# Lead of an attention and two-MLP kernel: copies spread over three engines, first products in halves

## The chip, the cores and the metric

One core of one Trainium2 chip. The metric is the device time of one execution in microseconds. The median of three runs of the kernel before is 594.18 us (593.97 to 595.03).

## The reference

For 2 batches, 8 heads, 768 positions and 64 dimensions a head, each query attends to the keys within 15 positions and to 24 block summaries (the maximum of each 32 keys; the mean of their 32 values). The result, 1536 tokens of 512, goes through two MLPs.

```python
scores_l_m = np.where(mask_l, scale * q @ k.T, -1e9)          # |i - j| < 16
scores_s = scale * q @ k_sum.T + np.log(block)
a = softmax(concat[scores_l_m, scores_s])
x = a @ concat[v, v_sum]                                       # (1536, 512)
h = np.maximum(x @ w_in, 0.0);  x = h * h @ w_out              # 512 -> 2048 -> 512
h = x @ w_in2;  return (h * sigmoid(h)) @ w_out2
```

The weights arrive as 8-byte numbers and are turned into 4-byte ones in the kernel.

## The kernel before, in words

Attention works in 24 tiles of 64 queries; a tile's scores are 4 head pairs of 128 partitions x 120 columns (96 keys of the window and 24 summaries). Every product of the MLPs is made of three passes over high and low halves of the operands (`split`). The first MLP runs over three blocks of 512 tokens, and each block over 16 chunks `s` of 128 hidden columns: `gemm1` (12 matmuls of 512 columns), relu and square on ScalarE, a split, `gemm2` (12 more). The second MLP follows.

The subject is the **lead**: the first 8 tiles (`NLEAD`), in two groups of 4 (`NGRP`). They give the 512 tokens of block 0, and before they are done no MLP product can start. Block 0's chunks are interleaved with tiles 8 to 15. A lead tile's steps, by the names in `first_order`:

- `kt`: one head pair's transposed keys from DRAM; `ksum` (L620, VectorE): their block maxima.
- `kwl` (L627, ScalarE): copies the 4 windows of a group, 128 x 384, out of `kt` into the score tile `kws`. Eight of them, (head pair, group).
- `ksl` (L632, VectorE): copies the summaries behind the windows, 128 x 96. Eight.
- `psl` (L641, PE) scores of one tile and head pair; `ttl` (L400, VectorE) adds the mask and takes the minimum; `exl` (L405, ScalarE) the exponential. 32 of each.
- `ze`, `rc`, `nt` (L425, L428, L436, VectorE): the sum's inverse and the product with it; `psa` (L442, PE) transposes; `a` (L449, ScalarE) copies out of PSUM.
- `vs` (L647, PE): value summaries of batch 0 into the PSUM tile `psv`; `vmean` (L651, ScalarE): copies them into `vlead` behind the values, 24 partitions x 2048, once for each group. `vfm` (L655, ScalarE): from there to two buffers of later tiles.
- `av` (L457, PE): attention times values; `xh` (L465, ScalarE) and `xl` (L468, VectorE): high and low part of the tokens, in `xt`.

A weight chunk's steps: `raw` (DMA, 512 KB), `sc` (L285, ScalarE), `sh` (L290, VectorE), `st2` (L293, VectorE), `hi` (L703, ScalarE), `lo` (L706, VectorE); `scr` stores the joined `wo` chunk. There are 5 buffers for raw chunks (`NRAW`), and a load waits for the `st2` five chunks earlier.

Every engine runs its instructions in program order, and so does SP, which issues the loads and stores. The program order of block 0 is made by `first_order` (L63): a list scheduler. Each step has an engine, a cost, a due time and what it depends on. It takes the engine step that can start earliest, and of the steps of that engine which can start by then the one with the earliest due time. It doesn't look ahead: a step that is ready goes before one that is more urgent and ready a moment later. The plan's times only make the order; on the chip the waits decide. GpSimd has no step in it before.

`FILL` (L47) puts 6 and 4 idle matmuls behind two of the early scores, and `WARM` 10 at the start.

Of the kernel before, what the change touches and what calls it, by code (L numbers as in the profile page):

```python
# [10 lines left out]
F32 = mybir.dt.float32  # L11
# [11 lines left out]
P = 128  # L23
# [3 lines left out]
QT = 64  # L27
NWIN = QT + 2 * WIN
NK = NWIN + NSUM
TPB = S // QT  # L30
NG = B * TPB
NHP = H // 2
NF = DFF // P
# [10 lines left out]
NVF = 2  # L44
NLEAD = 8
NGRP = 4
# [6 lines left out]
NRING = 8  # L53
FIRST2 = 1
DEC1 = 14
GROUPS = [[(0, 0, 256, 256, 0), (1, 256 * 0, 128, 128, 256)], [(1, 256, 384, 128, 0), (2, 0, 256, 256, 128)]]
STARTS = [[0, 128, 512, 256, 384, 640], [768, 1024, 1152, 896, 1280, 1408]]
CHAIN = ["11", "s1", "s2", "s4", "s3", "12", "22"]
# [4 lines left out]
def first_order():  # L63
# [6 lines left out]
    def op(eng, name, arg, dur, due, deps=(), bank=None, kb=0):  # L70
        o = index[name, arg] = dict(eng=eng, name=name, arg=arg, dur=dur, due=due + shift.get(name, 0), deps=list(deps), bank=bank, kb=kb,
                                    n=len(ops))
        ops.append(o)
# [4 lines left out]
    def tile_due(g):  # L78
        return 0.25 * g if g < NLEAD else 46 + 11 * (g - NLEAD)
# [9 lines left out]
    for hp in range(NHP):  # L89
        op("vec", "ksum", hp, 1.0, -50 + hp, [("kt", hp, 0)])  # L90
        for i in range(NLEAD // NGRP):
            op("act", "kwl", (hp, i), .5, -50 + hp + 51 * i, [("kt", hp, 0)])
            op("vec", "ksl", (hp, i), .13, -50 + hp + 48 * i, [("ksum", hp, 0)])
    for c in range(6):
        op("pe", "vs", c, .92, 2.7 + .1 * c, [("vr", c // 2, 0)])
    for i in range(NLEAD // NGRP):
        op("act", "vmean", i, 1.9, -5, [("vs", c, M) for c in range(6)] + [("vl", i, 0)] * 0)
    for i in range(NVF):
        op("act", "vfm", i, .6, tile_due(NLEAD) - 10 + i, [("vmean", 0, 0)])

    for j in range(4 * NHP):
        due = tile_due(TPB) - 20 + j
# [5 lines left out]
    for g in range(NFIRST):  # L108
        due, two = tile_due(g), g - 2 >= NLEAD
        if g < NLEAD:  # L110
            for hp in range(NHP):
                op("pe", "psl", (g, hp), .29, due, [("kwl", (hp, g // NGRP), A), ("ksl", (hp, g // NGRP), A), ("q", g // NGRP, 0)] +
                   [("psl", (g, hp - 1), 0)] * (hp > 0), bank=None if hp else ("acc", "ttl", (g, NHP - 1)))
                op("vec", "ttl", (g, hp), .21, due, [("psl", (g, hp), M), ("cst", 0, 0)])
                op("act", "exl", (g, hp), .385, due, [("ttl", (g, hp), A)])
            exp = [("exl", (g, hp), A) for hp in range(NHP)]
        else:
            load("kw", g, 246, due - 9, [("pss", g - 2, M)] * two)
            load("qr", g, 131, due - 8.9, [("pss", g - 2, M)] * two)
            load("vf", g, 196, due - 6, [("av", g - 2, M)] * two)  # L120
            op("vec", "kwc", g, .13, due - .5, [("kw", g, 0)] + [("kvr", 4 * NHP - 1, 0)] * (g >= TPB))
            if TPB <= g < TPB + NVF:
                op("vec", "vfc", g, .35, due, [("vf", g, 0), ("vendc", 0, A)])
            op("pe", "pss", g, 1.22, due, [("kwc", g, A), ("qr", g, 0)] + [("gemm1", 1, 0)] * (g == NLEAD), bank=("att", "ttr", g))
            op("vec", "ttr", g, .84, due, [("pss", g, M), ("psa", g - 2, M)])
            op("act", "exp", g, 1.54, due, [("ttr", g, -.45)])
            exp = [("exp", g, A)]
        op("vec", "ze", g, .09, due, exp)
        op("vec", "rc", g, .1, due, [("ze", g, .1)])
        op("vec", "nt", g, .78, due, [("rc", g, .1)])  # L130
        op("pe", "psa", g, .62, due - 2, [("nt", g, -.1)], bank=("att", "a", g))
        op("act", "a", g, .56, due, [("psa", g, M)] + [("av", g - 1, M)] * (g > NLEAD))
        values = [("vl", g // NGRP, 0), ("vmean", g // NGRP, A)] if g < NLEAD else [("vf", g, 0), ("vfm", g % NVF, A)]
        op("pe", "av", g, .66, due, values + [("a", g, A)] + [("vfc", g, A)] * (TPB <= g < TPB + NVF),
           bank=("acc" if g < NLEAD else "att", "xl", g))
        op("act", "xh", g, .32, due, [("av", g, M)])
        op("vec", "xl", g, .36, due, [("xh", g, A)])

    chunks = [(x, s) for s in range(NF) for x in ("wi", "wo")]
    for i, (x, s) in enumerate(chunks):  # L140
        due = chunk_due(s) - 5 + .5 * (x == "wo") - 20 * (not i)
        load("raw", (x, s), 524, chunk_due(s) - 14 + .5 * (x == "wo") - 100 * (not i),
             [("st2", chunks[i - NRAW], A)] if i >= NRAW else [])
        before = [("sc", chunks[i - 1], 0)] * (i > 0)
        if i >= NSPL:
            y = chunks[i - NSPL]
            before += [("lo", y, A)] + [("scr", y[1], 0)] * (y[0] == "wo")
        op("act", "sc", (x, s), .59, due, [("raw", (x, s), 0)] + before)
        op("vec", "sh", (x, s), .35, due, [("raw", (x, s), 0)])
        op("vec", "st2", (x, s), .61, due, [("sh", (x, s), 0), ("sc", (x, s), A)])  # L150
        if x == "wo":
            load("scr", s, 262, chunk_due(s) + 2, [("st2", (x, s), A)])
        op("act", "hi", (x, s), .57, due, [("st2", (x, s), A)] + [("gemm2", s - NWO - NXWO, M)] * (x == "wo" and s >= NWO + NXWO))
        op("vec", "lo", (x, s), .61, due, [("hi", (x, s), A)])

    for s in range(NF):
        due = chunk_due(s)
        op("pe", "gemm1", s, 2.72, due, [("xl", g, A) for g in range(NLEAD)] + [("lo", ("wi", s), A)] +
           [("relu", s - 2, A)] * (s >= 2))
        op("act", "relu", s, .57, due, [("gemm1", s, M)] + [("gl", s - 2, A)] * (s >= 2))  # L160
        op("act", "sq", s, .57, due, [("relu", s, 0)])
        op("act", "gh", s, .57, due, [("sq", s, 0)] + [("gemm2", s - 3, M)] * (s >= 3))
        op("vec", "gl", s, .61, due, [("gh", s, A)])
        op("pe", "gemm2", s, 2.72, due + 5 * LAG, [("gl", s, A), ("lo", ("wo", s), A)] + [("gemm2", s - 1, 0)] * (s > 0))

    free = dict(sp=0.0, act=0.0, vec=0.0, pe=5.6)
    end, banks, moved = {}, dict(att=[], acc=[]), 2.0
    room = dict(att=2, acc=4)

# [34 lines left out]
def kernel(  # L204
# [35 lines left out]
    def copy(eng, o, i, scale=1.0):  # L240
        if eng is act:
            return act.activation(out=o, in_=i, func=AF.Copy, scale=scale)  # L242
        return eng.tensor_copy(out=o, in_=i)  # L243
# [48 lines left out]
    def dec_join(name, c):  # L292
        vec.scalar_tensor_tensor(out=c, in0=c, scalar=3, in1=raws.pop(name)[:, :, 0],  # L293
                                 op0=ALU.logical_shift_left, op1=ALU.bitwise_or)
# [255 lines left out]
    def gemm1(w, x, c0, n, h):  # L550
        for k in range(NKC):
            ws = slice(k * P, (k + 1) * P)
            xh, xl = x[:, 0, k, c0:c0 + n], x[:, 1, k, c0:c0 + n]
            mm(h, w[:, 0, ws], xh, start=(k == 0), stop=False)
            mm(h, w[:, 0, ws], xl, start=False, stop=False)
            mm(h, w[:, 1, ws], xh, start=False, stop=(k == NKC - 1))
# [16 lines left out]
    def first_block():  # L573
# [50 lines left out]
        def kwl(hpi):  # L624
            hp, i = hpi
            w = kts[hp][:, i * NGRP * QT:i * NGRP * QT + NWIN]
            copy(act, kws[i][hp // 2][:, hp % 2, :, 0:NWIN], bass.AP(w.tensor, w.offset, [w.ap[0], [QT, NGRP], w.ap[1]]))  # L627

        def ksl(hpi):
            hp, i = hpi  # L630
            s = ksum[0][:, hp]
            copy(vec, kws[i][hp // 2][:, hp % 2, :, NWIN:NK], bass.AP(s.tensor, s.offset, [s.ap[0], [0, NGRP], s.ap[1]]))  # L632

        def psl(ghp):
            g, hp = ghp
# [12 lines left out]

        def vmean(i):
            means = psv[NWIN:NK]  # L650
            copy(act, vlead[NWIN:NK, i * NGRP:i * NGRP + NGRP].rearrange("p g h d -> p g (h d)"),  # L651
                 bass.AP(means.tensor, means.offset, [means.ap[0], [0, NGRP], means.ap[1]]))

        def vfm(i):
            copy(act, vf[i][NWIN:NK], vlead[NWIN:NK, 0])  # L655

        def kv(j):
            hp, w, i = j // 4, j // 2 % 2, j % 2
# [27 lines left out]
        def name(xs):  # L686
            return f"{xs[0]}{xs[1]}"
# [17 lines left out]
        def lo(xs):  # L705
            sub(vec, ws[xs][:, 1], cs[xs].bitcast(F32), ws[xs][:, 0].bitcast(F32))  # L706

        def gemm1_(s):
            h = hs[s] = ps_h.tile([P, 512], F32, tag="h", name=f"h0_{s}")
            gemm1(wi1[s], x, 0, 512, h)  # L710

        def relu(s):
            rs[s] = r_p.tile([P, 512], F32, tag="r", name=f"r0_{s}")
# [17 lines left out]
        def xh(g):  # L731
            if g * QT >= BLOCKS[0]:
# [6 lines left out]
                  exl=lambda a: exponential(*a), nt=lambda g: norm(g, vec),  # L739
                  psa=transposes, a=a_copy, av=products, xh=xh, xl=x_low, raw=raw, sc=sc,  # L740
                  sh=lambda xs: dec_low(name(xs)),
                  st2=lambda xs: dec_join(name(xs), cs[xs]), scr=scr_, hi=hi, lo=lo, gemm1=gemm1_, relu=relu, sq=sq, gh=gh,
                  gl=gl, gemm2=gemm2_)
        for what, arg in first_order():
            do[what](arg)
# [363 lines left out]
```

## Time and profile before

| | us |
|---|---|
| median of three runs | 594.18 |
| the profiled execution's own time | 595.07 |
| its span, first to last instruction | 593.3 |
| PE busy | 584.0 |
| VectorE busy | 388.7 |
| ScalarE busy | 367.1 |
| GpSimd busy | 88.9 |

The profiled execution is 0.89 us above the median; 1.77 us of it lie around the span. PE is TensorE's matmul row, DVE is VectorE, ACT is ScalarE, POOL is GpSimd, SP is the engine that issues DMAs. A row's "x4" counts instructions, and merged timeline rows add the lengths from the first start to the last end. On VectorE and ScalarE an instruction's recorded length runs somewhat into the next one's start, so that the spacing of starts is what one more costs.

### The profile page before, as it was taken

How to read it: one execution, taken by the hardware profiler on the slowest of the kernel's cores; microseconds unless marked ns; L12 is line 12 of the kernel's file. 1: busy time of each engine (PE TensorE's matmuls, PEld its weight loads, DVE VectorE, ACT ScalarE, POOL GpSimd, SP SyncE). 2: the span in 40 equal slices, each digit the busy share in tenths (PEclk: the TensorE clock that was granted, in tenths of full speed). 3: DMA queues.
4: the chain of work that ended last, by engine and by line, in shares of the span. 5: the costliest groups of instructions: out<-in, count | busy, mean ns of one | idle time of the engine just before them, and what ended most of it. 6: DMA issues, size and time to landing. Idle time of an engine off the chain costs nothing.

```text
span 593.3 us, 9499 instructions
## 1 busy us (share of the span) xinstructions
PE 584.0 (98%) x3300; PEld 491.9 (83%) x3300; DVE 388.7 (66%) x975; ACT 367.1 (62%) x848; POOL 88.9 (15%) x93
## 2 busy tenths in 40 slices
PE   7989999999999999999999999999999999999997
PEld 6578888887887887888888898999988998889995
DVE  5989999733756665267544676777776766666542
ACT  5999998654555655375553676566656655555532
POOL 0000000012554443156333300000000000000000
PEclk9999999999999999999999999999999999999999
DMA  8999999525598888526682112242229411111102
GB/s 308 270 290 352 345 360 339 185 83 181 189 345 303 284 269 303 211 107 206 233 274 68 36 36 89 88 144 88 84 89 378 174 39 36 31 25 35 36 19 106
DMA packets 42240, 104.42 MB, mean 176 GB/s; under 512 B 4560, under 2 KB 11856, under 8 KB 42192
## 3 DMA queue, kind: packets, MB, share of 16 engines
q1 hardware_dynamic: 42192, 103.81, 51.4%
q8 instruction: 26, 0.43, 0.3%
q14 instruction: 22, 0.18, 0.1%
HBM read 78.37 MB, written 25.43 MB: 175 GB/s over the span
## 4 chain that ended last, share of the span: by engine, by line
PE 95%; ACT 2%; DMA 1%; DVE 1%; issue 0%; SPq 0%; DVEq 0%
PE acc L238 45%; PE h L238 23%; PE hx L238 11%; PE hz L238 6%; PE pss L238 4%; PE hy L238 3%; PE psa L442 2%; PE av L238 2%; DMA t_ksum<-in_kT_dram 1%; ACT T L405 1%; PE psv L238 1%; ACT vlead L242 1%; ACT a L242 0%; ACT xt L242 0%; PE idle_out L238 0%; DVE ksum L620 0%
## 5 line engine op out<-in xcount | busy, mean ns | idle before, releaser
L238 PE MATMUL acc<-wq,g 128*128 128x512 f32 x576 | 142.4, 392 | 0.0
L238 PE MATMUL h<-xt,wi 128*128 128x512 f32 x576 | 142.2, 394 | 0.0
L238 PE MATMUL acc<-g,wo 128*128 128x512 f32 x576 | 141.1, 393 | 0.0
L238 PEld LDWEIGHTS acc<-g,wo 128*128 128x128 f32 x576 | 107.1, 188 | 23.1 <-ACT xt L242 0.2
L238 PEld LDWEIGHTS h<-xt,wi 128*128 128x128 f32 x576 | 106.3, 188 | 22.9 <-issue 0.6
L238 PEld LDWEIGHTS acc<-wq,g 128*128 128x128 f32 x576 | 107.1, 188 | 19.7 <-DVE wq L246 0.2
L246 DVE TENSOR_TENSOR g<-r,g 128x512 fp32r<-128x512 f32 x48 | 38.4, 801 | 60.5 <-ACT g L242 31.0
L246 DVE TENSOR_TENSOR r_s<-v,r_s 128x256 fp32r<-128x256 f32 x48 | 20.5, 431 | 50.2 <-ACT r_s L242 50.1
L242 ACT ACTIVATE g<-s 128x384 fp32r<-128x384 f32 x64 | 33.2, 521 | 22.0 <-DVE s L246 22.0
L246 DVE TENSOR_TENSOR g<-s,g 128x384 fp32r<-128x384 f32 x64 | 35.5, 556 | 15.1 <-ACT g L242 13.2
L405 ACT ACTIVATE T<-T,m 128x120 f32<-128x120 f32 x96 | 36.7, 384 | 11.2 <-DVE m L400 11.0
L242 ACT ACTIVATE e<-hx 128x384 f32<-128x384 f32 x32 | 15.7, 492 | 43.8 <-PE hx L238 43.8
L238 PE MATMUL hx<-x_t,r_s 128*128 128x384 f32 x192 | 38.9, 337 | 0.0
L238 PEld LDWEIGHTS hx<-x_t,r_s 128*128 128x128 f32 x192 | 34.5, 188 | 2.7
L932 ACT ACTIVATE s<-e 128x384 f32<-128x384 f32 x48 | 25.2, 525 | 15.4 <-DVE e L246 15.3
L246 DVE TENSOR_TENSOR s<-e,s 128x384 f32<-128x384 f32 x48 | 26.5, 553 | 5.2 <-ACT s L932 5.2
L526 ACT ACTIVATE r<-h 128x512 f32<-128x512 f32 x16 | 9.5, 596 | 30.9 <-PE h L238 30.9
L246 POOL TENSOR_TENSOR wo<-c_wo,wo 128x512 fp32r<-128x512 f32 x16 | 26.1, 1632 | 13.1 <-ACT wo L242 12.6
L242 ACT ACTIVATE r<-u 128x256 fp32r<-128x256 f32 x48 | 19.5, 409 | 12.7 <-PE hx L238 12.7
L243 POOL COPY qd<-qr 128x256 f32<-128x256 f32 x8 | 5.8, 719 | 133.7 <-DVE z L425 125.8
L400 DVE CUSTOM_DVE_ANT_0 T<-pss,cst_sb 128x120 f32<-128x120 f32 x96 | 21.8, 274 | 4.3 <-PE pss L238 4.0
L246 POOL TENSOR_TENSOR r<-r 128x512 f32<-128x512 f32 x16 | 17.0, 1064 | 48.6 <-ACT g L531 48.6
(112 smaller groups left out, 912.0 us busy)
## 6 DMA issues: line engine op xcount, KB each, us to landing
raw_wi<-in_w_in_dram SPq DMA_DIRECT2D x16, 512.0 KB, 5.6
raw_wo<-in_w_out_dram SPq DMA_DIRECT2D x16, 512.0 KB, 5.6
raw_wp<-in_w_out_dram SPq DMA_DIRECT2D x16, 512.0 KB, 5.4
split<-wo SPq DMA_DIRECT2D x16, 512.0 KB, 3.7
raw_wj<-in_w_in_dram SPq DMA_DIRECT2D x16, 512.0 KB, 4.6
wo<-split SPq DMA_DIRECT2D x16, 512.0 KB, 3.4
c<-scr_dram SPq DMA_DIRECT2D x32, 256.0 KB, 2.6
scr_dram<-c_wo SPq DMA_DIRECT2D x16, 256.0 KB, 4.4
```

Of the source, the lines that this page charges most:

```text
L238: pe.matmul(o, l, r, **kw)
L242: return act.activation(out=o, in_=i, func=AF.Copy, scale=scale)
L243: return eng.tensor_copy(out=o, in_=i)
L246: return eng.tensor_tensor(out=o, in0=a, in1=b, op=op)
L400: vec.tensor_tensor_reduce(out=d["T"][:, c], in0=d["ps"][:, c], in1=cst_sb[:, kind * NK:kind * NK + NK], scale=-0.125, scalar=3.0e38, op0= ...
L405: act.activation(out=d["T"][:, c], in_=d["T"][:, c], func=AF.Exp, bias=d["m"][:, c:c + 1], scale=-1.0, accum_out=d["z"][:, c:c + 1])
L442: pe.transpose(ps[0:NK, c], d["T"][:, c], id_sb)
L526: act.activation(out=r, in_=h, func=AF.Relu)
L932: act.activation(out=s, in_=src, func=AF.Sigmoid)
```

## The change

GpSimd becomes an engine of the plan. Seven of the eight `kwl` go from ScalarE to GpSimd (the first stays), all eight `ksl` from VectorE to GpSimd, both `vfm` from ScalarE to GpSimd, and the second `vmean` from ScalarE to VectorE. The first MLP product of chunks 0 and 1 is made in two halves of 256 tokens: `half1` needs only tiles 0 to 3, `gemm1` makes the rest. The chunks are ordered anew, the `wo` of a chunk 1.5 places behind its `wi` (`wi0, wi1, wo0, wi2, wo1, wi3, ...`), and the decoding of every chunk from the third on waits, in the plan, for the last lead tile's `nt`. Several of the plan's costs are changed.

```diff
+NHALF = 2
         for i in range(NLEAD // NGRP):
-            op("act", "kwl", (hp, i), .5, -50 + hp + 51 * i, [("kt", hp, 0)])
-            op("vec", "ksl", (hp, i), .13, -50 + hp + 48 * i, [("ksum", hp, 0)])
+            op("pool" if i or hp else "act", "kwl", (hp, i), .5, -50 + hp + 51 * i, [("kt", hp, 0)])
+            op("pool", "ksl", (hp, i), .25, -50 + hp + 48 * i, [("ksum", hp, A)])
     for i in range(NLEAD // NGRP):
-        op("act", "vmean", i, 1.9, -5, [("vs", c, M) for c in range(6)] + [("vl", i, 0)] * 0)
+        op("vec" if i else "act", "vmean", i, 2.2 if i else 1.85, -5, [("vs", c, M) for c in range(6)])
     for i in range(NVF):
-        op("act", "vfm", i, .6, tile_due(NLEAD) - 10 + i, [("vmean", 0, 0)])
+        op("pool", "vfm", i, .7, tile_due(NLEAD) - 10 + i, [("vmean", 0, 0)])
-                op("pe", "psl", (g, hp), .29, due, [("kwl", (hp, g // NGRP), A), ("ksl", (hp, g // NGRP), A), ("q", g // NGRP, 0)] +
+                op("pe", "psl", (g, hp), 0.2, due, [("kwl", (hp, g // NGRP), A), ("ksl", (hp, g // NGRP), A), ("q", g // NGRP, 0)] +
...
-        op("act", "a", g, .56, due, [("psa", g, M)] + [("av", g - 1, M)] * (g > NLEAD))
+        op("act", "a", g, .5, due, [("psa", g, M)] + [("av", g - 1, M)] * (g > NLEAD))
...
-        op("pe", "av", g, .66, due, values + [("a", g, A)] + [("vfc", g, A)] * (TPB <= g < TPB + NVF),
+        op("pe", "av", g, .53, due, values + [("a", g, A)] + [("vfc", g, A)] * (TPB <= g < TPB + NVF),
...
-    chunks = [(x, s) for s in range(NF) for x in ("wi", "wo")]
+    chunks = sorted(((x, s) for s in range(NF) for x in ("wi", "wo")), key=lambda c: c[1] + 1.5 * (c[0] == "wo"))
+        held = [("nt", NLEAD - 1, 0)] * (i > 1)
-        op("act", "sc", (x, s), .59, due, [("raw", (x, s), 0)] + before)
-        op("vec", "sh", (x, s), .35, due, [("raw", (x, s), 0)])
-        op("vec", "st2", (x, s), .61, due, [("sh", (x, s), 0), ("sc", (x, s), A)])
+        op("act", "sc", (x, s), .57, due, [("raw", (x, s), 0)] + before + held)
+        op("vec", "sh", (x, s), .35, due, [("raw", (x, s), 0)] + held)
+        op("vec", "st2", (x, s), .6, due, [("sh", (x, s), 0), ("sc", (x, s), A)])
-        op("pe", "gemm1", s, 2.72, due, [("xl", g, A) for g in range(NLEAD)] + [("lo", ("wi", s), A)] +
-           [("relu", s - 2, A)] * (s >= 2))
+        if s < NHALF:
+            op("pe", "half1", s, 1.45, due - 30, [("xl", g, A) for g in range(NGRP)] + [("lo", ("wi", s), A)])
+        op("pe", "gemm1", s, 1.45 if s < NHALF else 2.72, due, [("xl", g, A) for g in range(NLEAD)] + [("lo", ("wi", s), A)] +
+           [("half1", s, 0)] * (s < NHALF) + [("relu", s - 2, A)] * (s >= 2))
-    free = dict(sp=0.0, act=0.0, vec=0.0, pe=5.6)
+    free = dict(sp=0.0, act=0.0, vec=0.0, pool=2.0, pe=5.6)
...
+        def half1(s):
+            h = hs[s] = ps_h.tile([P, 512], F32, tag="h", name=f"h0_{s}")
+            gemm1(wi1[s], x, 0, 256, h[:, 0:256])
+
         def gemm1_(s):
-            h = hs[s] = ps_h.tile([P, 512], F32, tag="h", name=f"h0_{s}")
-            gemm1(wi1[s], x, 0, 512, h)
+            if s < NHALF:
+                gemm1(wi1[s], x, 256, 256, hs[s][:, 256:512])
+            else:
+                h = hs[s] = ps_h.tile([P, 512], F32, tag="h", name=f"h0_{s}")
+                gemm1(wi1[s], x, 0, 512, h)
```

In `kwl`, `ksl`, `vmean` and `vfm` only the engine of the copy changes, and `half1` joins the table of steps.

## Rows read from the trace of the kernel before

**Rows 1.** Page, parts 1 and 2: busy time by engine; the granted clock by slice.

```profile
PE 584.0 (98%) x3300; PEld 491.9 (83%) x3300; DVE 388.7 (66%) x975; ACT 367.1 (62%) x848; POOL 88.9 (15%) x93
...
PEclk9999999999999999999999999999999999999999
```

**Rows 2.** Windows: stretch, its length, each engine's busy time (instructions), clock, DMA share, GB/s.

```profile
9.12:31.06 21.94, 19.57 (x159) 12.43 (x159) 19.81 (x126) 20.51 (x79) 0.00 (x0) 1.00 1.05 304
31.06:37.44 6.38, 5.70 (x147) 5.17 (x146) 4.57 (x15) 6.32 (x14) 0.00 (x0) 1.00 0.94 260
60.00:80.00 20.00, 20.00 (x114) 16.11 (x113) 19.35 (x53) 18.12 (x40) 0.00 (x0) 1.00 0.99 350
```

**Rows 3.** Chain that ended last, in order of time: start, length, what.

```profile
28.99 3.63 ACT vlead L242 x2
36.22 1.22 PE pss L238 x16
37.44 5.67 PE h L238 x24
...
47.24 2.72 PE h L238 x12
...
333.75 1.06 PE hx L238 x6
```

**Rows 4.** ScalarE's groups from 9.7 to 29 us (columns as in the page's part 5).

```profile
L242 ACT ACTIVATE kws<-t_ksum 128x384 f32<-128x384 f32 x4 | 1.9, 510 | 0.0
```

**Rows 5.** Timeline of ScalarE: start, length, what, [idle before it <- releaser].

```profile
9.72 0.39 ACT L405 ACTIVATE T<-T,m 128x120 f32<-128x120 f32 x1 [0.55 <-DVE m L400]
...
14.80 0.38 ACT L405 ACTIVATE T<-T,m 128x120 f32<-128x120 f32 x1
...
15.18 0.38 ACT L405 ACTIVATE T<-T,m 128x120 f32<-128x120 f32 x1
...
36.01 0.64 ACT L242 ACTIVATE xt<-av 128x256 fp32r<-128x256 f32 x2
...
39.99 0.63 ACT L242 ACTIVATE vfr<-vlead 24x512 f32<-24x512 f32 x1
```

**Rows 6.** Timeline of VectorE.

```profile
8.17 0.95 DVE L620 TENSOR_REDUCE ksum<-t_ksum 128x24 f32<-128x768 f32 x1 [2.99 <-DMA t_ksum<-in_kT_dram]
...
11.76 0.33 DVE L243 COPY kws<-ksum 128x96 f32<-128x96 f32 x2
...
29.87 0.43 DVE L290 TENSOR_SCALAR raw_wi<-raw_wi 128x512 int32<-128x512 int32 x1 [0.48 <-DMA raw_wi<-in_w_in_dram]
30.21 0.85 DVE L436 TENSOR_SCALAR T<-T,r 128x120 f32<-128x120 f32 x4
...
36.75 0.75 DVE L246 TENSOR_TENSOR xt<-av,xt 128x256 fp32r<-128x256 f32 x2
...
50.22 0.68 DVE L246 TENSOR_TENSOR wi<-c_wi,wi 128x512 fp32r<-128x512 f32 x1
```

**Rows 7.** PE's waits: who waited for whom, total us, times, longest.

```profile
PE psa L442 <- DVE T L436: 1.4, 1, 1.4
```

**Rows 8.** GpSimd's groups over the whole span, shapes kept apart.

```profile
L246 POOL TENSOR_TENSOR wo<-c_wo,wo 128x512 fp32r<-128x512 f32 x16 | 26.1, 1632 | 13.1 <-ACT wo L242 12.6
L246 POOL TENSOR_TENSOR r<-r 128x512 f32<-128x512 f32 x16 | 17.0, 1064 | 48.6 <-ACT g L531 48.6
...
L243 POOL COPY qd<-qr 128x256 f32<-128x256 f32 x8 | 5.8, 719 | 133.7 <-DVE z L425 125.8 <-issue 4.4 <-PE pss L238 3.4
```

**Rows 9.** VectorE's groups over the whole span, shapes kept apart.

```profile
L290 DVE TENSOR_SCALAR raw_wp<-raw_wp 128x512 int32<-128x512 int32 x16 | 16.9, 1058 | 0.0
...
L290 DVE TENSOR_SCALAR raw_wo<-raw_wo 128x512 int32<-128x512 int32 x16 | 6.8, 424 | 1.1 <-DMA raw_wo<-in_w_out_dram 1.1
...
L243 DVE COPY xr<-acc 128x512 f32<-128x512 f32 x6 | 4.1, 689 | 4.6 <-PE acc L238 4.6
```

**Rows 10.** Timeline of PE.

```profile
52.88 3.00 PE L238 MATMUL h<-xt,wi 128*128 128x512 f32 x12
```

More of the change, by code (lines that the diff above doesn't have):

```diff
@@ L626, in kwl @@
             w = kts[hp][:, i * NGRP * QT:i * NGRP * QT + NWIN]
-            copy(act, kws[i][hp // 2][:, hp % 2, :, 0:NWIN], bass.AP(w.tensor, w.offset, [w.ap[0], [QT, NGRP], w.ap[1]]))
+            copy(pool if i or hp else act, kws[i][hp // 2][:, hp % 2, :, 0:NWIN], bass.AP(w.tensor, w.offset, [w.ap[0], [QT, NGRP], w.ap[1]]))
         def ksl(hpi):
@@ L631, in ksl @@
             s = ksum[0][:, hp]
-            copy(vec, kws[i][hp // 2][:, hp % 2, :, NWIN:NK], bass.AP(s.tensor, s.offset, [s.ap[0], [0, NGRP], s.ap[1]]))
+            copy(pool, kws[i][hp // 2][:, hp % 2, :, NWIN:NK], bass.AP(s.tensor, s.offset, [s.ap[0], [0, NGRP], s.ap[1]]))
         def psl(ghp):
@@ L650, in vmean @@
             means = psv[NWIN:NK]
-            copy(act, vlead[NWIN:NK, i * NGRP:i * NGRP + NGRP].rearrange("p g h d -> p g (h d)"),
+            copy(vec if i else act, vlead[NWIN:NK, i * NGRP:i * NGRP + NGRP].rearrange("p g h d -> p g (h d)"),
                  bass.AP(means.tensor, means.offset, [means.ap[0], [0, NGRP], means.ap[1]]))
         def vfm(i):
-            copy(act, vf[i][NWIN:NK], vlead[NWIN:NK, 0])
+            copy(pool, vf[i][NWIN:NK], vlead[NWIN:NK, 0])
         def kv(j):
@@ L741, in first_block @@
                   sh=lambda xs: dec_low(name(xs)),
-                  st2=lambda xs: dec_join(name(xs), cs[xs]), scr=scr_, hi=hi, lo=lo, gemm1=gemm1_, relu=relu, sq=sq, gh=gh,
+                  st2=lambda xs: dec_join(name(xs), cs[xs]), scr=scr_, hi=hi, lo=lo, half1=half1, gemm1=gemm1_, relu=relu, sq=sq, gh=gh,
                   gl=gl, gemm2=gemm2_)
```

## The prediction

> **What bounds the kernel now.** I read the page first. PE is busy 98% of the span and its granted clock is full from the lead to the end [rows 1]; by the chain of waits, from 36.22 us on everything is PE, product after product [rows 3]. What remains to be won is therefore the time before that. The windows show it: from 9.12 to 31.06 us VectorE is busy 19.81 of 21.94 us and ScalarE 20.51, GpSimd not at all; from 31.06 to 37.44 ScalarE is busy 6.32 of 6.38 us [rows 2]. The chain names ScalarE's two `vmean` copies, 3.63 us one behind the other, as the step ahead of the last values' products [rows 3]. They can't start before the last exponential, because ScalarE is full up to there. VectorE is nearly as full, but waits for weights with urgent work behind: the shift of a raw chunk waits 0.48 us for its DMA with the last tile's `nt` queued after it, and PE waited 1.4 us for that `nt` [rows 6, 7]. After 37 us the other engines stay full (VectorE 19.35 of 20 us from 60 to 80) while PE never waits [rows 2].
>
> So the time of the change is: how much earlier PE's unbroken stretch begins, less what the halves cost, less what PE must wait later.
>
> **The change part by part.**
>
> *ScalarE.* In its first-exponential-to-last-`xh` stretch it holds 20.51 us up to 31.06 and then, until the `xh` that end at 36.65, 5.59 more [rows 2, 5]: 26.1 us. It loses four `kwl` (1.9 us [rows 4]; the other three stand before 9.72, where it waits for data) and one `vmean` (half of 3.63, 1.8 us): 22.4 us are left. The first exponential at 9.72 had waited 0.55 us for the minimum [rows 5], and VectorE made two `ksl` ahead of that; without them I put it at 9.45. The last `xh` is then at 31.9 plus waits.
>
> *The waits that replace the copies.* GpSimd must do what was spread over two engines. Its price for a 128 x 384 copy is in no row. From above: the `qd` copy of 256 elements takes 719 ns, so 384 take 1.08 us. From below: `r<-r` reads two operands of 512 in 1064 ns, 1.04 ns per element read, so 384 take 0.40 us [rows 8]. The `qd` copy is the nearest in kind, but steps through its source, and `kwl` reads straight runs of 96; I take 0.7, between the two. `ksl`, a quarter as long, I put at 0.25 us by the same scale.
>
> The second head pair's keys are there at 8.17 [rows 6]. As the plan takes what is ready first, the windows of *both* groups go ahead of the summary copies, whose maxima come later. For head pair 2 I count five window copies and two summary copies: 8.2 + 5 x 0.7 + 2 x 0.25 = 12.2, its own summaries until 12.45, against 12.1 now [rows 6]; for head pair 3 another window copy and two summary copies later, 13.7. Meanwhile ScalarE has the eight exponentials of head pairs 0 and 1, 8 x 0.38 = 3.05 us by the spacing of starts [rows 5], which end at 12.5. With 0.6 us from summaries to exponential it waits about 0.6 us for pair 2 and again for pair 3: 1.3 us together. Each 0.1 us on a copy adds about 0.6 us, since six stand ahead. At 0.40 us a copy the wait is gone, at 1.08 it is 3.6 us. Last `xh`: 31.9 + 1.3 = 33.2; last `xl` 0.4 us later.
>
> *VectorE.* It loses six `ksl` (two take 0.33 us [rows 6]: 1.0 us) and, as `sh` of the third chunk is now held, 0.4 us [rows 9]. It gains the second `vmean`, 24 x 2048 out of PSUM. From above: 4 x 689 ns, the copy of 512 out of PSUM [rows 9], 2.76 us; from below ScalarE's 1.8. I take 2.3. So 19.81 - 1.4 + 2.3 = 20.7 us behind 9.12, plus about 0.9 us of waits for late scores: the last `nt` and `vmean` are done at about 30.7, little earlier than now. But ScalarE is free then, and the chain from there (transposes, `a`, `av`, `xh`, `xl`) no longer stands behind two copies. With the eight `xl` behind that, 3.0 us by the last two's 0.75 [rows 6], VectorE ends the lead at about 33.8. This is the later of the two engines, and I take it: 3.6 us before the 37.4 of now.
>
> *Halves.* A 512-column product takes 2.72 us for 12, 227 ns each; 384 columns take 1.06 us for six, 177 each [rows 3]. Straight on, 256 columns take 127 ns: a half is 1.52 us, and two are 0.33 dearer than one whole; two chunks 0.65 us. From above: 177 ns, if no product gets shorter than the shortest of full height here, 2.12 us a half, 3.05 us in all. From below: half of the whole, nothing. The straight line is nearest. The first half of chunk 0 runs while the last four tiles finish, so 1.52 us of products are done before 33.8. On the other hand the scores of tile 9, 1.2 us, stand before 37.44 now [rows 3] and will be behind it.
>
> *What is moved and costs nothing.* The chunk order exchanges loads in SP's queue: the first five are the same chunks, with `wi1` in `wo0`'s place, and the sixth is `wi3` instead of `wo2`, which needs a buffer that `wi0` frees. No load is added. The stores `scr` shift with their `wo`, and loads queued behind them in SP with them; cover is the buffers ahead. GpSimd issues no DMA, so nothing is queued behind its copies but copies. `vfm` is read by tile 8's products, long after; if that cover went, it would cost one copy. The held steps queue nothing ahead of a wait.
>
> *Later.* PE comes about 3.3 us earlier, VectorE's remaining work only 2.5, since what was decoded between 31 and 37 us is left over. The split of chunk 3 is done at 50.90 and its product starts at 52.88 [rows 6, 10]: 2.0 us of slack, of which I use less than 1. I count nothing.
>
> **Sum:** 3.6 - 1.2 + 1.52 - 0.65 = 3.3 us. Against the profiled execution (595.07: span 593.3 and 1.77 around it) that is 591.8; it stands 0.89 above the median, and for the median I predict 594.18 - 3.3 = **590.9 us**.
>
> *A rule against the change.* In the rows a VectorE shift of 128 x 512 takes 424 ns in block 0, where GpSimd idles, and 1058 ns (`raw_wp`) in the block where it works; GpSimd's `wo` takes 1632 ns against 1064 for `r` of the same shape [rows 8, 9]. So the two do stretch each other. The Trainium skill, SBUF — State Buffer, § Who interferes with whom, says that GpSimd and a VectorE instruction in a two-port mode, or with two SBUF inputs, exclude each other for the whole instruction. By that rule the trace agrees, and the sum would stay if the copies are over before the `nt` begin; it would move to the third rival if they are not.
>
> **The rivals.**
>
> *1. Given back later.* The weights, not the tokens, hold PE between 37 and 60 us. For it: VectorE is full there and gains less than PE. Against: 2.0 us of slack. If it uses up the slack and waits 1.7 us, 594.18 - 1.6 = 592.6. Much the same time comes if the halves aren't where they help: the plan may put `half1` behind all of `av`, and then 1.52 us of cover is gone: 592.4.
>
> *2. Hidden.* Copies on GpSimd at the upper bound: 1.08 us, 2.3 us more waiting, a gain of 1.0: 593.2. Likewise halves at 177 ns: 3.3 - 2.4 = 0.9, 593.3. Somewhat dearer still, and nothing is left. For it: the only copy in the trace.
>
> *3. Slower.* GpSimd's copies become the bound of the lead: place, the scores of head pairs 2 and 3; price, six times what a copy takes over 0.7. It decides from 0.7 + 3.3 / 6 = 1.25 us a copy. At 1.08 stretched as `wo` is against `r` (1632 / 1064 = 1.53), 1.65 us, the wait grows by 5.7 us: 594.18 + 2.4 = 596.6. Against: VectorE's work in that stretch is mostly minima out of PSUM and reductions, not the shifts that stretched.
>
> *4. The change doesn't do what it says:* the second `vmean` waits on VectorE for PE's `vs`, earlier in program order than it should be, and `nt` of the last tiles queue behind it. ScalarE's gain of 1.8 us is then VectorE's loss: a gain of 1.5, 592.7.
>
> **How the numbers follow.** The forecast (a gain of 2 to 5 us) gets 0.50, the first rival 0.14, the fourth 0.10, the second 0.14, the third 0.12. A measurement of this kernel tells about 0.2%, 1.2 us, from no change. The forecast, the first and the fourth are faster by more; the second is within it, as is a little of the fourth; the third is slower: 0.73, 0.15, 0.12. The range: at its low end no wait for GpSimd (1.3) and halves for nothing (0.65), 594.18 - 5.25 = 588.9; at its high end the second rival and somewhat beyond, 593.9. The forecast's own is 588.9 to 592.2.
>
> **What would show it.** Right: GpSimd's window copies near 0.7 us; ScalarE waiting about a microsecond between 12 and 15 us and then full; one `vmean` on each engine side by side; the first half of chunk 0 before 33 us, the second near 34; afterwards no wait of PE. Wrong: window copies over 1 us, with PE and ScalarE idle from 11 to 16 us; VectorE idle ahead of its `vmean`; a half of over 1.6 us; PE waiting for `lo` of `wi` or for a `wo` between 37 and 60 us; a granted clock that falls in the lead, where PE now waits more.

## The result and the profile after

The changed kernel takes 598.37 us (median of four runs, 597.70 to 599.10) against 594.44 for the one before in the same runs: a ratio of 1.0066 (1.0048 to 1.0083), 3.9 us slower. 590.9 was predicted, with a range up to 593.9. The profiled execution took 597.7 us, its span is 595.9 us.

The page of the changed kernel, parts 1 and 2, against [rows 1]:

```profile
PE 586.4 (98%) x3324; PEld 495.0 (83%) x3324; DVE 392.8 (66%) x968; ACT 362.7 (61%) x838; POOL 95.8 (16%) x110
...
PEclk9979999999999999999999999999999999999999
```

The work has moved as the change says: ScalarE is busy 4.4 us less, VectorE 4.1 us more and GpSimd 6.9 us more. (Of VectorE's 4.1 us the moved copies are 0.6; 2.5 are the shifts of `raw_wp`, long after the lead.) One digit is new: the third slice, 29.8 to 44.7 us, in which TensorE's granted clock was not full. The timeline of PE in that place (line 242 is the matmul, 446 the transposes):

```profile
25.51 1.90 PE L242 MATMUL psv<-vrows,share 128*24 128x512 f32 x4
27.34 0.65 PE L446 MATMUL psa<-cst_sb,T 128*120 128x128 f32 x4
31.70 2.83 PE L242 MATMUL av<-a,vlead 120*64 120x64 f32 x48 [3.71 <-ACT vlead L246]
34.45 1.11 PE L446 MATMUL psa<-cst_sb,T 128*120 128x128 f32 x4
35.49 2.70 PE L242 MATMUL av<-a,vlead 120*64 120x64 f32 x64
38.12 1.70 PE L242 MATMUL h<-xt,wi 128*128 128x256 f32 x12
39.75 0.69 PE L242 MATMUL av<-a,vlead 120*64 120x64 f32 x16
40.36 7.33 PE L242 MATMUL h<-xt,wi 128*128 128x256 f32 x48
```

PE stands still for 3.71 us ahead of the first `av` and waits for ScalarE's value copy; its longest wait in the lead was 1.4 us before [rows 7]. The matmuls behind the stop are slow: 16 of `av` take 0.69 us at 39.75, but 48 take 2.83 at 31.70, and 1.62 in a run further below. The windows of the same kernel give the clock (columns as in [rows 2]):

```profile
15.00:22.00 7.00, 7.00 (x70) 4.80 (x66) 6.92 (x52) 5.24 (x21) 0.00 (x0) 1.00 1.05 244
...
25.00:30.00 5.00, 2.99 (x12) 1.08 (x12) 4.64 (x13) 2.92 (x13) 0.00 (x0) 1.00 1.02 386
30.00:35.00 5.00, 3.30 (x51) 3.19 (x52) 2.71 (x10) 4.44 (x7) 1.17 (x2) 0.50 1.07 288
35.00:40.00 5.00, 5.00 (x87) 4.46 (x87) 4.11 (x10) 3.93 (x9) 0.00 (x0) 0.81 0.87 297
```

After PE's stop the granted clock is 0.50, the lower level of 1.2 GHz; PE works again from 31.70, and the clock is back at 2.4 GHz in the stretch of 35 to 40: a mean of 0.81 over 5 us is 1.9 us at the lower level, so until about 36.9. It fell while PE stood still: taken by single microseconds, the granted clock is 1.00 from 29 to 30 us and 0.52 from 30 to 31. The row of 15 to 22 us matters further below.

Why PE stood still is in the two engines that copy the means. The timelines of VectorE and of ScalarE:

```profile
27.44 2.30 DVE L247 COPY vlead<-psv 24x2048 f32<-24x2048 f32 x1 [0.26 <-PE psv L242]
...
30.39 0.86 DVE L440 TENSOR_SCALAR T<-T,r 128x120 f32<-128x120 f32 x4
```

```profile
27.49 0.20 ACT L409 ACTIVATION_READ_ACCUMULATOR T<-T,m 128x1 f32 x1
29.77 1.87 ACT L246 ACTIVATE vlead<-psv 24x2048 f32<-24x2048 f32 x1 [2.08 <-DVE vlead L247]
```

Both copies read the PSUM tile `psv`. VectorE's copy, for tiles 4 to 7, goes first; ScalarE's, for tiles 0 to 3, waits 2.08 us for VectorE's end and then takes 1.87. The plan had put them 0.26 us apart and side by side. They run one after the other, and first the one that nobody needs yet. Tile 7's normalisation (30.39) stands behind VectorE's copy as well.

The window and summary copies that were moved to GpSimd did no harm here: PE has no wait for GpSimd in this run. GpSimd's groups from 0 to 13 us:

```profile
L247 POOL COPY kws<-t_ksum 128x384 f32<-128x384 f32 x7 | 3.4, 507 | 4.3 <-DMA t_ksum<-in_kT_dram 4.1
L247 POOL COPY kws<-ksum 128x96 f32<-128x96 f32 x8 | 1.9, 267 | 1.2 <-DVE ksum L624 1.1
```

### The profile page after: what moved, and what is told of

It is laid out like the page before. It is cut to its first block, busy times and chain, and to the rows that moved or that the text cites. A ratio compares the mean times of both kernels' runs of the same rounds, so it can differ in the third digit from the quotient of the medians.

```text
span 595.9 us, 9544 instructions
## 1 busy us (share of the span) xinstructions
PE 586.4 (98%) x3324; PEld 495.0 (83%) x3324; DVE 392.8 (66%) x968; ACT 362.7 (61%) x838; POOL 95.8 (16%) x110
## 4 chain that ended last, share of the span: by engine, by line
PE 98%; DVE 1%; ACT 0%; issue 0%; DVEq 0%
PE acc L242 45%; PE h L242 23%; PE hx L242 11%; PE hz L242 6%; PE pss L242 4%; PE hy L242 3%; PE av L242 3%; PE psa L446 2%; PE idle_out L242 1%; PE psv L242 1%; DVE vlead L247 0%; ACT vlead L246 0%; DVE ro L247 0%; DVE idle_in L585 0%; PE psv L677 0%
## 5 line engine op out<-in xcount | busy, mean ns | idle before, releaser
L242 PE MATMUL h<-xt,wi 128*128 128x512 f32 (+1 forms) x600 | 142.8, 386 | 0.0
L242 PEld LDWEIGHTS h<-xt,wi 128*128 128x128 f32 x600 | 107.5, 188 | 22.2 <-issue 0.6
L250 DVE TENSOR_TENSOR g<-r,g 128x512 fp32r<-128x512 f32 x48 | 37.1, 774 | 61.1 <-ACT g L246 31.0
L250 POOL TENSOR_TENSOR wo<-c_wo,wo 128x512 fp32r<-128x512 f32 x16 | 28.1, 1753 | 13.1 <-ACT wo L246 12.7
L246 ACT ACTIVATE a<-psa 120x512 f32<-120x512 f32 x24 | 14.2, 592 | 15.3 <-PE psa L446 15.1
```

The source lines that it names most:

```text
L242: pe.matmul(o, l, r, **kw)
L250: return eng.tensor_tensor(out=o, in0=a, in1=b, op=op)
```

## The experiments

Ratios are to the kernel before, measured beside each run on the same chip; times are medians. The kernel before stood at 594.4 us beside e1 to e4, at 595.1 beside e5, e7, e8 and e9, at 594.3 beside e6, e10 and e11 and at 594.4 beside e12 and e13; an expectation in microseconds was written against 594.4, so the ratios are what is compared. A ratio's interval is 0.1 to 0.2% to either side, 0.5 to 1.1 us.

### The first group's copy first, and the wait filled

```diff
-        op("vec" if i else "act", "vmean", i, ..., [("vs", c, M) for c in range(6)])
+        op("vec" if i else "act", "vmean", i, ..., [("vs", c, M) for c in range(6)] + [("vmean", 0, A)] * i)
```

> The changed kernel, with VectorE's copy of the value means for tiles 4 to 7 placed behind ScalarE's copy for tiles 0 to 3 in the plan. Theory A (the two copies read one PSUM tile, are made to wait for each other, and the wrong one goes first; PE's 3.7 us wait then halves its clock): ScalarE's copy starts at about 27.8 us instead of 29.8, the first values' products at 29.7 instead of 31.7, PE waits 1.7 us and its clock stays full; 595.2 us (3 us under the changed kernel). Theory B (the loss is in the held decoding and the new chunk order, not in the copies): less than 1 us, 597.5 to 598.5. Theory C (only VectorE's and ScalarE's own work counts, the order of the two copies is nothing, for the later one ends at the same time): 598.

The plan is made anew with this edit, so tile 7's normalisation, and with it its transposes, now come ahead of VectorE's copy too.

Measured: 595.01 us, ratio 0.9998 (0.9980 to 1.0015). The whole loss is gone. The timeline of PE of this kernel, then ScalarE's copy and the window of 30 to 35 us:

```profile
26.25 1.90 PE L242 MATMUL psv<-vrows,share 128*24 128x512 f32 x4
...
30.38 2.08 PE L242 MATMUL av<-a,vlead 120*64 120x64 f32 x64 [0.26 <-ACT vlead L246]
33.25 1.62 PE L242 MATMUL av<-a,vlead 120*64 120x64 f32 x48 [0.78 <-DVE xt L250]
34.80 1.68 PE L242 MATMUL h<-xt,wi 128*128 128x256 f32 x12
...
37.97 7.08 PE L242 MATMUL h<-xt,wi 128*128 128x256 f32 x46 [0.45 <-DVE wi L250]
```

```profile
28.46 1.87 ACT L246 ACTIVATE vlead<-psv 24x2048 f32<-24x2048 f32 x1
```

```profile
30.00:35.00 5.00, 3.96 (x114) 3.63 (x114) 4.94 (x9) 4.98 (x13) 1.17 (x2) 1.00 1.08 280
```

`av` starts 1.3 us earlier, and the clock is full. To price the clock alone, the wrong order was left and PE kept busy during the wait, by 16 idle matmuls ahead of tile 0's `av`:

```diff
+        if g == 0:
+            st["turn"](16)
...
         for h in range(H):
             mm(av[...], v[0:NK, h], a[0:NK, h * QT:(h + 1) * QT], start=True, stop=True)
```

> The changed kernel with 16 idle matmuls of 512 columns (3.5 us) ahead of the first values' products, where PE waits 3.7 us. Nothing else moves. Theory A with the clock as a cost of its own: the granted clock stays full through 30 to 37 us, the first values' products still start at 31.7, and the stretch from there to the last lead tile gets 2 to 2.5 us shorter: 596 us. Theory C (the half clock lies beside ScalarE's and VectorE's work, which sets the pace): within 0.5 us of the changed kernel, 598.

Measured: 596.1 us, ratio 1.0023 (1.0010 to 1.0036). The timeline of PE, and the window of 30 to 35 us:

```profile
28.22 3.92 PE L242 MATMUL idle_out<-idle_in 128*128 128x512 f32 x16
32.19 1.62 PE L242 MATMUL av<-a,vlead 120*64 120x64 f32 x48
33.74 0.65 PE L446 MATMUL psa<-cst_sb,T 128*120 128x128 f32 x4
34.32 2.08 PE L242 MATMUL av<-a,vlead 120*64 120x64 f32 x64
```

```profile
30.00:35.00 5.00, 4.95 (x84) 4.01 (x84) 3.26 (x12) 4.72 (x8) 1.17 (x2) 1.00 1.09 290
```

The clock is full, and the same 48, 4 and 64 matmuls take 1.62, 0.65 and 2.08 us instead of 2.83, 1.11 and 2.70: 2.3 us, though `av` starts half a microsecond later. So of the loss about 2.3 us are the clock and the rest, 1.3 us by the two starts of `av` (31.70 and 30.38), the wait itself. The ratios say the same within their intervals: from 1.0066 to 1.0023 are 2.6 us, from there to 0.9998 another 1.5.

### What makes one copy wait for the other

Both copies on ScalarE (no second engine at `psv`):

```diff
-        op("vec" if i else "act", "vmean", i, 2.2 if i else 1.85, ...)
+        op("act", "vmean", i, 1.85, ...)
```

> The changed kernel with both copies of the value means on ScalarE, as before. Theory A: first values' products at 29.7 us, second copy done at 31.5, no clock loss; VectorE is relieved of 2.3 us; 595 us, about as the first experiment. Theory B: 597.5 or more. If all other parts of the change are worth something, this lies under the kernel before (594.4); if they are worth nothing, on it; if they cost, over it.

Measured: 595.15 us, 1.0011 (0.9997 to 1.0025). In order on one engine is as good as in order on two.

`psv` read once, by ScalarE (`vmone`), then copies from SBUF on two engines, ScalarE's to tiles 1 to 3 and VectorE's to tiles 4 to 7:

```diff
+        def vmone(_):
+            copy(act, vlead[NWIN:NK, 0].rearrange("p h d -> p (h d)"), psv[NWIN:NK])
+
         def vmean(i):
-            means = psv[NWIN:NK]
+            means = vlead[NWIN:NK, 0].rearrange("p h d -> p (h d)")
+            lo, n = (NGRP, NGRP) if i else (1, NGRP - 1)
...
```

> The changed kernel, but the means are read from PSUM once (24 x 512, ScalarE, 0.6 us), and the seven other copies are made from that in SBUF: three on ScalarE (1.4 us), four on VectorE (1.1 to 2.2 us), side by side. Theory A: no engine waits for the other's copy (no row of ScalarE waiting for VectorE's vlead); both done by 30 us, first values' products at 29.8 us, clock full; 594 us or below. If the two copies still stand one behind the other, it isn't the shared PSUM tile that orders them but the tile that they write, and theory A falls in that point.

Measured: 595.83 us, 1.0018 (1.0005 to 1.0031), not the 594 or below that was expected. The timelines of ScalarE, VectorE and GpSimd:

```profile
28.26 0.59 ACT L248 ACTIVATE vlead<-psv 24x512 f32<-24x512 f32 x1
...
29.50 1.48 ACT L248 ACTIVATE vlead<-vlead 24x1536 f32<-24x1536 f32 x1
```

```profile
28.69 1.59 DVE L442 TENSOR_SCALAR T<-T,r 128x120 f32<-128x120 f32 x4
30.31 1.22 DVE L249 COPY vlead<-vlead 24x2048 f32<-24x2048 f32 x1
```

```profile
28.98 1.21 POOL L249 COPY vfr<-vlead 24x512 f32<-24x512 f32 x2 [16.20 <-ACT vlead L248]
```

The two copies write the same tile `vlead` and overlap from 30.31 to 30.98 without a wait. So it was not the written tile but the read one in PSUM that put them in a row. The Trainium skill, PSUM — Partial Sum Buffer, § PSUM bank collisions raise a hardware error, says that accesses of two engines to the same partitions of one bank must be kept apart; that agrees with the wait in the changed kernel, and no run here lets two engines in at once. The second thing to see is `nt` of tile 7, four instructions in 1.59 us, where the same four take 0.86: GpSimd's copies to the later tiles ran beside it.

### Where the predicted 3.3 us went

With the order mended the kernel is only as fast as before. So each part was taken out or put in alone. The moved copies alone, in the kernel before:

```diff
-            op("act", "kwl", (hp, i), ...)
-            op("vec", "ksl", (hp, i), ...)
-        op("act", "vfm", i, ...)
+            op("pool" if i or hp else "act", "kwl", (hp, i), ...)
+            op("pool", "ksl", (hp, i), ...)
+        op("pool", "vfm", i, ...)
...
```

> The kernel before with one part of the change alone: the copies of windows, key summaries and later tiles' value summaries on GpSimd; both value-summary copies stay on ScalarE, in their order, no halves, the old order of the chunks. Theory P (TensorE's own queue set the pace of the lead: in the trace of before it is busy 18.5 us of the 20 between 8 and 28 us, and waits 1.2 and 1.4 us there): what these copies free on ScalarE can give back at most those waits, so 0.5 to 1.5 us: 593 to 594. Theory S (ScalarE set the pace, as forecast; the gain is taken by the other parts): the lead ends 3 us earlier: 591 to 592.

Measured: 595.63 us, 1.0017 (0.9998 to 1.0035). Both theories expected a gain; none shows. The timelines of this kernel say why, ScalarE first and PE after it:

```profile
26.50 0.38 ACT L405 ACTIVATE T<-T,m 128x120 f32<-128x120 f32 x1
...
28.31 0.68 ACT L285 ACTIVATE c_wi<-raw_wi 128x512 f32<-128x512 f32 x1
29.08 3.63 ACT L242 ACTIVATE vlead<-psv 24x2048 f32<-24x2048 f32 x2
```

```profile
27.14 1.90 PE L238 MATMUL psv<-vrows,share 128*24 128x512 f32 x4
...
31.00 2.08 PE L238 MATMUL av<-a,vlead 120*64 120x64 f32 x64 [1.38 <-ACT vlead L242]
```

ScalarE is done with the exponentials 2 us earlier (the last starts at 26.50 us instead of 28.49; in the kernel before the copies began right behind it, at 28.99 [rows 3]). But the copies need the last `psv` product, and that ends at 27.14 + 1.90 = 29.04 us, so ScalarE fills the time with weights and the copies begin at 29.08. In the kernel before it is not different; a row of ScalarE's timeline there and one of PE's, which the prediction doesn't show:

```profile
28.49 0.38 ACT L405 ACTIVATE T<-T,m 128x120 f32<-128x120 f32 x1
26.76 1.90 PE L238 MATMUL psv<-vrows,share 128*24 128x512 f32 x4
```

`psv` was complete at 28.66, 0.33 us before the copies. However empty ScalarE was, the copies could begin only as much earlier as TensorE's own queue came to that product.

Does VectorE or TensorE set that queue's pace? One kernel leaves out VectorE's addition of 1e-9 to the sums of the lead's eight tiles, the other the four idle matmuls behind the second group of scores, both with the copies in order:

```diff
-        op("vec", "ze", g, .09, due, exp)
+        if g >= NLEAD:
+            op("vec", "ze", g, .09, due, exp)
...
```

```diff
-FILL = {(NGRP - 1, 0): 6, (NGRP - 1, 1): 4}
+FILL = {(NGRP - 1, 0): 6}
```

> The changed kernel with the first group's copy first (595.0 us), without VectorE's addition of 1e-9 to the sums of the lead's eight tiles: 8 x 0.16 = 1.3 us of VectorE's work less in the lead, nothing else. Theory V (VectorE sets the lead's pace): about 1 us faster, 594.0, with the first products of tile 0 before 29.6 us instead of 30.4. Theory P (TensorE's queue sets it): no difference, 594.8 to 595.1.

> The changed kernel with the first group's copy first (595.0 us), without the four idle products of TensorE that follow the second group of scores (1.2 us at 10.3 us): TensorE has about 1 us less work in the lead. Theory P (TensorE's queue sets the lead's pace): its later work starts earlier, the first products of tile 0 at 29.4 instead of 30.4 us, and 594.0 us in all. Theory V or S (VectorE or ScalarE sets it): TensorE waits as much longer, 595.0 us.

Measured: 1.0001 (0.9986 to 1.0016) and 1.0006 (0.9991 to 1.0021): neither gains, as far as intervals of 0.9 us to either side can tell a gain of 1 us from none. The waits of PE up to 60 us, first without the addition, then with less filling:

```profile
PE av L243 <- ACT vlead L247: 1.2, 1, 1.2
...
```

```profile
PE pss L242 <- POOL kws L247: 1.4, 1, 1.4
...
PE av L242 <- DVE xt L250: 1.7, 1, 1.7
```

With VectorE relieved, PE comes to tile 7's transposes a microsecond earlier (28.32 instead of 29.31 us) and waits 1.2 us for ScalarE's copy instead of 0.26. With TensorE relieved, PE waits 1.4 us at the same place for GpSimd, which copies windows and summaries from 9.24 to 11.71 us with hardly a pause. (The profiled execution of this kernel, 596.6 us, is 1.3 us above its median, so its later waits may be longer than usual.) The stop only moves. My theory that TensorE's queue alone bounds the lead is thereby no more right than that VectorE does.

The halves, and the new order of the chunks, each taken back:

```diff
-NHALF = 2
+NHALF = 0
```

> The changed kernel with the first group's copy first (595.0 us), and gemm1 of the first two chunks whole again. If half a product covers 0.87 us net (1.52 less 0.65), as forecast: 595.9. If its start behind the products of tile 6 and behind the low half of the second chunk makes it cover nothing: 0.65 us faster, 594.3.

```diff
-    chunks = sorted(((x, s) for s in range(NF) for x in ("wi", "wo")), key=lambda c: c[1] + 1.5 * (c[0] == "wo"))
+    chunks = [(x, s) for s in range(NF) for x in ("wi", "wo")]
-        held = [("nt", NLEAD - 1, 0)] * (i > 1)
+        held = []
```

> The changed kernel with the first group's copy first (595.0 us), with the old order of the chunks (wi and wo in turn) and without the wait of all chunks but the first two for the lead's last normalisation. If this part carries a gain of its own: slower than 595.0 by more than 0.5 us. If the sum of TensorE's waits is what counts and this part only moves them: 594.7 to 595.5.

Measured: 1.0000 (0.9988 to 1.0013) without halves and 1.0003 (0.9992 to 1.0013) with the old order. Neither part is worth anything that can be measured. The forecast for the halves, 0.87 us net, would have made their removal a ratio of about 1.0013 (0.9998 + 0.87 / 594), at the interval's edge.

### Can the rest be won?

PE's last waits in the kernel without halves, 28 to 37 us, are 2.6 us and hang on tile 7's normalisation, the value copies and the tokens. Two kernels without halves read the means once on ScalarE and let idle GpSimd spread them to the other seven tiles, one with `psv` earlier in PE's order and one without:

```diff
-        op("vec" if i else "act", "vmean", i, ..., [("vs", c, M) for c in range(6)] + [("vmean", 0, A)] * i)
+        if not i:
+            op("act", "vmone", 0, .55, -5, [("vs", c, M) for c in range(6)])
+        op("pool" if i else "pool", "vmean", i, 2.4 if i else 1.8, -5, [("vmone", 0, A)])
...
```

> The changed kernel without halves (594.9 us); the means' products of TensorE stand earlier, ScalarE reads the means out of PSUM once (0.55 us), and GpSimd spreads them to the other seven tiles, in two copies of about 1.8 and 2.4 us. ScalarE is relieved of 1.3 us and VectorE of 2.3 us at the end of the lead. Theory P (only TensorE's waits can be won, and those left at 28 to 36 us, 2.7 us in the kernel without halves, hang on these two copies): 1 to 2 us faster, 593 to 594. Rival: GpSimd's copies hold VectorE up (a normalisation of 0.85 us took 1.59 us beside GpSimd's copies in the run that read PSUM once), and the waits stay: 594.9 or more.

> As the kernel that spreads on GpSimd, with the means' products where the change has them. ScalarE's read of the means starts at 28 us, the first spread ends at 30.4, the second at 32.8. Theory P: TensorE waits for the first spread (about 1 us) and the second: 594.5 to 595.2; less than 0.3 us from the kernel without halves.

Measured: 598.05 us, 1.0065 (1.0053 to 1.0078), and 598.49 us, 1.0076 (1.0063 to 1.0089): as slow as the change, and the rival is right; the second was expected within 0.3 us of the kernel without halves. In the second, GpSimd, VectorE and PE:

```profile
28.67 3.35 POOL L249 COPY vlead<-vlead 24x1536 f32<-24x1536 f32 x2 [16.23 <-ACT vlead L248]
```

```profile
28.38 3.72 DVE L442 TENSOR_SCALAR T<-T,r 128x120 f32<-128x120 f32 x4
```

```profile
32.16 0.33 PE L448 MATMUL psa<-cst_sb,T 128*120 128x128 f32 x1 [1.51 <-DVE T L442]
```

The normalisation that takes 0.86 us by itself takes 3.72 beside 3.35 us of GpSimd's copies, almost as if the two took turns. The windows of this kernel show the granted clock once more:

```profile
30.00:35.00 5.00, 2.88 (x66) 2.33 (x66) 5.00 (x8) 2.08 (x5) 3.34 (x4) 1.00 1.07 281
35.00:40.00 5.00, 2.45 (x50) 1.96 (x51) 5.00 (x13) 4.19 (x11) 0.00 (x0) 1.00 0.91 300
40.00:45.00 5.00, 5.00 (x16) 3.92 (x15) 3.25 (x8) 1.77 (x3) 0.00 (x0) 0.66 0.91 291
```

PE was busy for 5.3 of 10 us at a full clock, and then, at work again, had 0.66 of it. The late copies cost their wait and afterwards the clock, as in the changed kernel.

Last, VectorE reads the means once and copies from SBUF, to all seven tiles (the diff) or, in the second kernel, to tiles 1 to 3, with ScalarE copying the rest; GpSimd's copies to later tiles come behind the lead in the plan:

```diff
-            op("act", "vmone", 0, .55, ...)
-        op("pool" if i else "pool", "vmean", i, 2.4 if i else 1.8, ...)
+            op("vec", "vmone", 0, .6, ...)
+        op("vec", "vmean", i, 1.3 if i else .95, ...)
...
```

> The changed kernel without halves (594.9 us; TensorE's waits between 28 and 37 us are 2.7 us there); VectorE alone copies the means: once out of PSUM (about 0.6 us), then from SBUF to the other seven tiles (about 0.9 and 1.2 us; seven tiles' worth took 2.7 us on two engines in the run that read PSUM once). ScalarE is relieved of 1.9 us where it is the last to be waited for, VectorE pays 0.4 us more, and GpSimd's two copies for the later tiles come behind the lead. Theory B (no engine alone bounds the lead; what is won is TensorE's waits, and one engine's relief moves the wait to the next): 0.3 to 1.5 us faster, 593.5 to 594.6, the waits of 28 to 37 us shrink to 1.2 to 2.4 us. Rival (VectorE is the bound at the end of the lead): 595.2 or more.

> As the kernel in which VectorE alone copies the means, with the copy to tiles 4 to 7 on ScalarE, from SBUF (24x2048, about 1.9 us), behind the first tile's high half. Theory B: 0 to 1 us faster than that kernel, 593 to 594.3, since the two engines now share the work without sharing a PSUM tile. Rival (ScalarE's order bounds the end of the lead): 0.5 us slower than it.

Measured: 596.14 us, 1.0033 (1.0021 to 1.0045), and 594.80 us, 1.0005 (0.9996 to 1.0013). With all of it on VectorE the kernel is slower; shared, it is the time of before. The copies of the first in VectorE's timeline, then GpSimd's:

```profile
27.37 0.70 DVE L249 COPY vlead<-psv 24x512 f32<-24x512 f32 x1 [0.27 <-PE psv L244]
28.10 1.75 DVE L249 COPY vlead<-vlead 24x1536 f32<-24x1536 f32 x1
```

```profile
28.20 1.17 POOL L249 COPY vfr<-vlead 24x512 f32<-24x512 f32 x2 [16.04 <-DVE vlead L249]
```

The copy of 1536 was put at 0.9 us and took 1.75, and PE waited 1.1 us for it ahead of `av` of tile 1. GpSimd's copies were not behind the lead: the plan only orders them, GpSimd had nothing ahead of them, and they ran from 28.20 to 29.37 us, beside that copy. So these two runs don't price VectorE's copies without GpSimd beside them. No version tried is faster than the kernel before. Untried is `psv` earlier in TensorE's order with the copies left on ScalarE and VectorE: e10 moved it, but with GpSimd's copies on top.

## Why the prediction was wrong

**The step that failed** is "The second `vmean`, 24 x 2048 out of PSUM", with its sign of success "one `vmean` on each engine side by side". The price was right: 2.30 us measured, 2.3 put. That they run side by side was wrong: two readers of one PSUM tile went one after the other, in the plan's order, the later group first. The fourth rival saw the place (the copy stands too early on VectorE) but took only ScalarE's 1.8 us off the gain and kept 1.5, 592.7, because it looked only at what queues behind VectorE's copy on VectorE, not at the other reader of `psv`. That the copy's wait would stop PE for 3.7 us, and that the granted clock would fall after it (named among the signs of being wrong, without a price), makes up the 3.9 us between before and after; e1, whose one edit is the order, takes all of it away.

**"They can't start before the last exponential, because ScalarE is full up to there"** is the step that lost the gain. It names one of two conditions. The other, the end of `psv` on PE at 28.66 us, stood 0.33 us from the same place, and the prediction gives it no time: the fourth rival alone names `vs`, for VectorE's copy (the end came to 27.41 in the changed kernel, 1.25 us earlier, and to 29.04 with the copies alone); PE's timeline from 11.35 us to 29.2 has a single wait, of 0.16 us. ScalarE was indeed full [rows 2] and was indeed relieved (5.24 us busy of the 7 from 15 to 22; PE, in the same row, 7.00 of 7), but PE and VectorE were as full. The copies moved only as that end did: they begin at 28.46 us in e1, where `psv` ends at 28.15, and at 29.08 with the copies alone. `av` gains 1.0 us with the copies in order (30.38 against 31.37 us) and 0.4 when the copies alone are moved (31.00); what this is more than the copies' own shift comes from tile 7's normalisation, for which PE had waited 1.4 us before [rows 7].

**The 3.6 us of the sum** ("VectorE ends the lead at about 33.8") is the term that came out short. It had VectorE done with tile 7's `nt` and its copy at 30.7 us and put the eight `xl`, 3.0 us, straight behind. In e5, with the copies in order and without halves, VectorE's timeline has them here:

```profile
29.89 2.30 DVE L247 COPY vlead<-psv 24x2048 f32<-24x2048 f32 x1
...
33.55 0.68 DVE L297 SCALAR_TENSOR_TENSOR c_wo<-c_wo,raw_wo 128x512 int32<-128x512 int32 x1
...
34.81 0.68 DVE L297 SCALAR_TENSOR_TENSOR c_wi<-c_wi,raw_wi 128x512 int32<-128x512 int32 x1
...
35.41 0.75 DVE L250 TENSOR_TENSOR xt<-av,xt 128x256 fp32r<-128x256 f32 x2
```

The copy ends at 32.19 us, 1.5 later than put, since it comes behind ScalarE's; and from there to the end of the last `xl` at 36.16 it is 4.0 us instead of 3.0, since two steps of decoding weights (33.55 and 34.81) stand between them. In the kernel before the last `xl` ends at 37.50 [rows 6], so the lead ends 1.3 us earlier instead of 3.6. The ninth tile's scores, which move behind it, take 1.2 us of that, as forecast. What is left is 0.1 us by one profile of each, and e5 measured 1.0000.

**Point by point.** GpSimd's window copies: 0.7 us put, 0.51 measured, so the third rival, from 1.25 us on, is out. A summary copy: 0.25 put, 0.27 measured. Half a product: 127 ns a matmul put; 48 matmuls, 36 of them half and 12 whole, take 7.33 us, which leaves (7.33 - 12 x 0.227) / 36 = 128 ns. What the halves cover: 1.52 us put; but the first half starts at 34.80 even in e1, behind `av` of tile 6 in program order, not before 33. Without halves PE waits 0.9 us for the tokens there, with them 0.45 for the second chunk's weights: the cover, about half a microsecond, is what the dearer halves cost (0.65). The first exponential: 9.45 put, 8.18 measured; that it was early changed nothing, since the end is set elsewhere. ScalarE's waits for late scores: 1.3 us put, 0.8 measured between 9 and 16 us; the second of the two didn't follow from the prediction's own numbers (13.7 + 0.6 = 14.3, but pair 2's four exponentials would last from 13.05 to 14.6), and the sum went by VectorE. "Given back later" is out: PE has no wait from 40 to 60 us in the changed kernel, and none from 38 to 60 in e1.

**The rule about GpSimd** that was weighed against the change, the Trainium skill's SBUF — State Buffer, § Who interferes with whom, was not what made it slower: the window copies were over at 12.3 us. Where copies did meet the normalisations, in e4 and in the runs that spread the means on GpSimd, the trace agrees with it (1.59 and 3.72 us against 0.86).

**What stays open** is which engine bounds the lead when the copies are in order. Relieving VectorE, TensorE or ScalarE one at a time moved the wait and won nothing that could be measured; a run that relieves all three wasn't made.

## What to carry to other kernels

Before a copy is put on a second engine, look at what both read: here two readers of one PSUM tile ran in program order, and the one whose result is needed first must then come first; reading it once and copying from SBUF let them overlap, though it made this kernel no faster. Before a busy engine is relieved, list everything that the step at its end waits for and how far each stood from being the last; here the second condition was 0.33 us away, and beyond that the copies began as much earlier as that one moved, and no more. A stop of TensorE is to be priced with the clock after it: here a stop of 3.7 us, which put the next products off by 1.3, brought 2.3 us of slow matmuls on top.

## What was not expected of the hardware

VectorE copies 24 x 2048 in 1.22 us from SBUF, 2.30 us from PSUM, but 24 x 1536 from SBUF in 1.75 us, longer than the larger copy, in e12 and e13 alike. That is 1.14 ns an element, the pace of PSUM (1.12) and not of the larger copy (0.60). GpSimd copied beside it both times; whether that or the copy's form is the cause isn't shown. GpSimd copies 128 x 384 in 0.51 us, less than the 0.7 that was put between two rows of before. And GpSimd's and VectorE's work on SBUF hardly went on side by side: beside 3.35 us of copies a normalisation of 0.86 us lasted 3.72, of which 0.37 lie outside the copies.
